# Two attention layers with memory and two gated FFNs on one core: one p-times-v run per unit, weights by columns, eight pooled PSUM banks, and a new order

## The chip, the core and the metric

The kernel runs on one core of one Trainium2 chip. A core has five engines with a queue each: TensorE (PE, its weight loader shown as PEld), VectorE (DVE), ScalarE (ACT), GpSimd (POOL) and SyncE (SP, which issues most DMAs). An engine takes its instructions in the order of its queue; semaphores hold an instruction back until what it needs is there. The metric is device time in microseconds (us), the median of several runs.

## The reference

The input is one sequence of S = 2048 rows of D = 512 numbers. Two layers follow each other, each an attention block A and a feed-forward block B with residuals; both layers use the same weights.

```
x = x + A(layernorm(x));  x = x + B(layernorm(x))      # twice

A: q, k, v = x@wq, x@wk, x@wv        # 32 heads of 16, 4 segments of 512 rows
   per segment s and head:
     p     = softmax(q k^T * scale + causal mask)      # inside the segment
     a_dot = p @ v
     a_mem = (phi(q) @ M) / (phi(q) @ z + 1e-6)        # M, z: of the segments before
     o     = g * a_mem + (1 - g) * a_dot
     M, z  = M + phi(k)^T v, z + sum(phi(k))           # phi(t) = t+1 if t > 0 else exp(t)
   return o @ wo
B: return (silu(x@w_gate) * (x@w_up)) @ w_down         # 512 -> 1792 -> 512
```

## The kernel before, in words

**Precision.** A product of two matrices is made of three matmuls of a faster 32-bit kind: each operand is split in a high and a low part (ACT copies the high part, DVE or POOL subtracts), and high x high, high x low and low x high are added in PSUM (`mm3`, matmuls at line 282). p times v and the memory update run in full 32 bits (four passes).

**Attention.** A layer has 4 segments x 4 groups of 8 heads x 2 halves = 32 units of four heads, `u = 0..31`. Per group, `qk_proj` projects q and k (line 282), ACT copies them to `raw` (468), POOL splits them into the tile `nat` (469, 471), and SP writes `nat` to DRAM (483, 484), from where `load3` brings it back per unit with heads side by side (`cq`, `ck`, lines 508, 513). Per unit there are then:

- `mx_units`: scores for the row maxima. For each of four heads, three fills of a PSUM bank `pmx` (line 531; key widths 256 and 256 in one bank, then 384, then 512), each followed by a masked maximum on DVE (538). `fin` transposes the 16 columns of maxima (547), and ACT sends them by DMA into a row of `cq` (549).
- `at_units`: ten transposed score blocks of 128 keys x 128 queries for four heads (`lt`, line 575, bank `plt`); ACT takes the exponential into tiles `p0`, `p1`, `pc` (581), POOL zeroes the upper triangle of the four diagonal blocks (585); then p times v.
- `pv`, lines 590 to 609: the array is used as four groups of 32 columns (mode "cols"), one head each. `pv(0)` does the first row of key blocks, 512 columns; `pv(1)` the remaining 384 + 128 + 256. Between the two stand three more score blocks. DVE transposes and scales the result (616 to 620).

Besides these, per group: `mem_read` (653), `mem_update` (transposes 669, then 16 small matmuls in mode "cols", 681; DVE and POOL add to M, 685 and 689); per segment: layernorm (`ln_pre`, `ln_fin`, transposes at 373), `v_proj` and `wo_proj` (282).

**FFN.** The first and last parts of the hidden dimension are done plainly (`up`, 975, `down`, 1049); the others by a scheme that needs seven instead of eight block products (`strassen`, 1005), with combinations of weights made on POOL (858, 872) and of inputs on DVE (`make_t`, 919). `down` adds to the residual on DVE (1054).

**Order.** Nothing runs in the order of the code. Each operation is recorded with an engine, a cost and a priority (`at(...)` sets it; the tables `OFF`, `PRE`, `EP`, `PAIR`, `STEP` shift kinds of work against each other, in units of 15 to 17 us), and `Program.issue` (148) then plays all engines: at each step it issues the operation with the lowest priority number among those that its model holds ready, where `LAT` gives the assumed delay from one engine to another and `DRAIN` the assumed cost of a change of mode on PE. What comes out is the order of each queue. No priority is looked at on the chip.

**PSUM.** Eight banks. Before, each had an owner: three `plt` in turn, two `pmx` in turn, one `ppv`, and two `pj` for all else, of which the planner gives the one that is free first. FFN products use the same names.

**Weights at the start.** `load_w4` (415) loads each of wq, wk, wv, wo in four DMAs of 128 rows x 512 columns and splits each piece. A projection of one group of heads needs 128 columns of all four pieces.

Of the kernel before, what the change touches and what calls it, by code (L numbers as in the profile page):

```python
# [12 lines left out]
OP = mybir.AluOpType  # L13
# [11 lines left out]
NB = 3  # L25
LPW = 3
WOT = ("pmx_0", "pmx_1", "pj", "pj")
EARLY_AT = (23, 25, 26)
PAIR, STEP, WAT, TAT = 13.0, 1.83, -2.5, (-1.0, -0.5)
T3E = "dve"  # L30
FIN = 1.9
WQ1 = -6.0
TA, TF = 15.0, 16.7
OFF = {'qe': (0.481, 1.468), 'at': (0.3, 1.1), 'mx': (-0.666, 0.16), 'lf': (-0.709, -0.318), 'mr': (0.865, 0.781), 'mu': (0.556, 0.139), 'wo': (0.263, 1.746), 'qk': (-0.342, 0.41), 'v': (-0.3, 0.518), 'lp': (0.034, 1.108)}
PRE = {'c': -1.851, 'mb': 0.212, 'lv': -1.7, 'lo': -0.87, 'gate': -1.0, 'v': -1.534, 'dv': 0.12, 'qk1': -1.2, 'mx': -1.0}
EP = {'w': -1.935, 'wn': 0.178, 'ln': -3.0, 'dn': -0.06, 'up': -2.73}
POOL_W = ""
TABLE = 1.28
DRAIN = {("full", "cols"): 0.195, ("cols", "full"): 0.095}
# [3 lines left out]
    pe=dict(pe=0.01, act=0.2, dve=0.2, sp=0.19),  # L43
    act=dict(act=0.22, dve=0.13, pe=0.27, pool=0.2, sp=0.15),
    dve=dict(dve=0.13, act=0.13, pe=0.25, pool=0.16, sp=0.12),
    pool=dict(pool=0.1, dve=0.06, pe=0.13, act=0.1, sp=0.05),
# [4 lines left out]
class Buf:  # L51
    def __init__(self, prog, pool, tag, shape, dtype):
# [4 lines left out]
        self.slot = None  # L57
        self.prev = None
# [9 lines left out]
class Op:  # L68
    __slots__ = ("table", "mode", "post", "eng", "cost", "lat", "fn", "prio", "bufs", "succ", "deps", "ready", "need", "wait", "index")

    def __init__(self, eng, cost, lat, fn, prio, bufs):
        self.eng, self.cost, self.lat, self.fn, self.prio, self.bufs = eng, cost, lat, fn, prio, bufs
        self.mode, self.table, self.post = None, None, 0.0
        self.succ, self.deps, self.ready, self.need, self.wait = [], set(), 0.0, None, 0


class Program:
# [19 lines left out]
    def op(self, eng, cost, fn, reads=(), writes=(), lat=0.0):  # L97
# [38 lines left out]
        for b in touch:  # L136
# [3 lines left out]
            if b.tag in self.shared:  # L140
                o.need = b
# [6 lines left out]
    def issue(self):  # L148
        for b in {id(b): b for o in self.ops for b in o.bufs if b.tag in self.shared}.values():
# [15 lines left out]
        held = {tag: [] for tag in self.shared}  # L165
        for o in self.ops:
            if o.wait == 0:
                heapq.heappush(fut[o.eng], (o.ready, o.index, o))
        done, bus, table, mode = 0, 0.0, "exp", "full"
        while done < len(self.ops):  # L170
            best = None
            for e in engs:
                f, n = fut[e], now[e]
                while True:
# [3 lines left out]
                    if n:  # L178
                        o = n[0][2]
                        b = o.need  # L180
                        if b is not None and b.slot is None:
                            if not free[b.tag]:
                                heapq.heappop(n)
                                held[b.tag].append(o)
                                continue
                            fr = min(free[b.tag])
                            if fr[0] > t[e] + 1e-9:
                                heapq.heappop(n)
                                o.ready = fr[0]
# [18 lines left out]
            b = o.need  # L208
            if b is not None and b.slot is None:
# [36 lines left out]
def infini_swiglu(ctx: ExitStack, tc: tile.TileContext, x, wq, wk, wv, wo, beta, wg, wu, wd, out,  # L246
# [149 lines left out]
    def attention(lay, x_in, x_out, slots, T, hook):  # L396
# [7 lines left out]
        def at(v):  # L404
            P.prio = base + v * T
# [800 lines left out]
```

## Time and profile before

| | us |
|---|---|
| median of 3 runs | 1937.13 (1933.95 to 1937.19) |
| span of the profiled execution | 1931.2 |
| PE busy | 1870.8 |
| DVE busy | 1406.9 |
| POOL busy | 905.9 |
| ACT busy | 873.0 |

The profiled execution is known by its span, from its first instruction to its last; the 5.9 us between it and the median of the runs are what lies around the span and what runs differ by. In a group's row stand: the line, the engine, the operation, what it writes and reads, the shapes, the count, then busy time and the mean of one in ns, then the idle time of the engine just ahead of it and what ended that. The first layer's attention fills about 0 to 530 us, its FFN to about 970, then the same again.

### The profile page before, as it was taken

What the parts mean: (1) busy time and instruction counts of PE and PEld (TensorE: products, weight loads), DVE (VectorE), ACT (ScalarE), POOL (GpSimd) and SP (SyncE); (2) the same over time, 40 slices, a digit from 0 to 9 for tenths busy, and PEclk for the clock granted to TensorE, in tenths of its full rate; (3) what the DMA queues carried; (4) which work ended last, traced back from release to release, by engine and by line L of the source; (5) the groups of instructions that cost most, each with busy time, mean ns of one, the idle gap of its engine ahead of it and who ended that gap; (6) DMA issues with size and microseconds to landing.
All of it is one profiled execution on the core that took longest, in us unless ns stands there. A gap on an engine that the chain in (4) does not pass through costs nothing.

```text
span 1931.2 us, 32319 instructions
## 1 busy us (share of the span) xinstructions
PE 1870.8 (97%) x11104; PEld 1437.2 (74%) x11104; DVE 1406.9 (73%) x3834; ACT 873.0 (45%) x1634; POOL 905.9 (47%) x1185
## 2 busy tenths in 40 slices
PE   7999999999989999999999999999999999999999
PEld 5677677776668887788867777777766788878887
DVE  5877867778777668766777678777797756686656
ACT  4555454555624343334326555555455334333332
POOL 5333443444546553655534334444355365455461
PEclk9999999999999999999999999999999999999999
DMA  7433434456131122221364344344561321221121
GB/s 235 135 111 124 132 116 146 129 151 195 45 136 50 55 72 82 71 61 44 95 215 121 102 133 132 116 149 132 152 188 39 131 66 44 87 77 51 44 60 44
DMA packets 120819, 206.09 MB, mean 107 GB/s; under 512 B 14160, under 2 KB 43856, under 8 KB 120656
## 3 DMA queue, kind: packets, MB, share of 16 engines
q1 hardware_dynamic: 118608, 203.49, 34.8%
q8 instruction: 89, 1.46, 0.3%
q10 hardware_dynamic: 2048, 0.53, 0.1%
q14 instruction: 74, 0.61, 0.1%
HBM read 136.34 MB, written 67.11 MB: 105 GB/s over the span
## 4 chain that ended last, share of the span: by engine, by line
PE 78%; DVE 8%; issue 4%; DMA 4%; POOL 3%; ACT 2%; SPq 0%; ACTq 0%; DVEq 0%; POOLq 0%
PE pj L282 16%; PE pj L1049 14%; PE plt L1005 11%; PE pmx L531 8%; PE pmx L1005 8%; PE ppv L603 7%; PE plt L575 6%; PE ppv L1005 3%; DVE junk L538 2%; DMA ck<-scrk 1%; PE pj L975 1%; PE pj L373 1%; PE pj L653 1%; DMA s<-nm 1%; POOL mem L858 1%
## 5 line engine op out<-in xcount | busy, mean ns | idle before, releaser
L538 DVE CUSTOM_DVE_ANT_0 junk<-pmx,amask 128x128 bf16<-128x128 f32 (+3 forms) x1024 | 458.7, 484 | 116.9 <-PE pmx L531 112.0
L282 PE MATMUL pj<-s,s 128*128 128x512 f32 x1416 | 488.2, 410 | 4.9 <-DVE s L1054 4.5
L1049 PE MATMUL pj<-s,vt 128*128 128x512 f32 x1296 | 414.4, 398 | 7.1 <-DVE s L1054 4.5
L581 ACT ACTIVATE s<-plt 128x512 f32<-128x512 f32 x512 | 284.2, 601 | 141.3 <-PE plt L575 133.3
L282 PEld LDWEIGHTS pj<-s,s 128*128 128x128 f32 x1416 | 263.9, 190 | 71.4 <-issue 24.9
L531 PE MATMUL pmx<-ck,s 127*128 127x256 f32 (+2 forms) x1024 | 299.1, 347 | 16.9 <-DVE mx L538 9.5
L1005 PE MATMUL plt<-s,s 128*128 128x512 f32 x1008 | 296.2, 396 | 3.4 <-ACT tt L1020 2.3
L1049 PEld LDWEIGHTS pj<-s,vt 128*128 128x128 f32 x1296 | 243.5, 189 | 68.9 <-DVE s L1054 8.0
L1054 DVE TENSOR_TENSOR s<-s,pj 128x512 f32<-128x512 f32 x224 | 152.9, 684 | 137.9 <-PE pj L1049 137.7
L575 PE MATMUL plt<-s,ck 128*128 128x256 f32 x1280 | 241.6, 288 | 4.2 <-DMA s<-nm 2.1
L531 PEld LDWEIGHTS pmx<-ck,s 127*128 127x128 f32 x1024 | 178.7, 190 | 88.8 <-DVE mx L538 27.0
L1005 PE MATMUL pmx<-s,s 128*128 128x512 f32 x720 | 239.2, 396 | 3.6 <-ACT s L871 2.4
L575 PEld LDWEIGHTS plt<-s,ck 128*128 128x128 f32 x1280 | 211.2, 189 | 32.7 <-ACT s L581 8.5
L1005 PEld LDWEIGHTS plt<-s,s 128*128 128x128 f32 x1008 | 189.6, 189 | 50.4 <-ACT tt L1020 2.7
L585 POOL TENSOR_SCALAR_AFFINE_SELECT s<-s 128x512 f32<-128x512 f32 x192 | 126.9, 664 | 186.5 <-ACT s L581 180.1
L1005 PEld LDWEIGHTS pmx<-s,s 128*128 128x128 f32 x720 | 135.5, 189 | 36.4 <-ACT s L871 3.2
L603 PE MATMUL ppv<-s,vt 128*32 128x512 f32 (+2 forms) x1536 | 136.8, 458 | 0.0
L872 POOL TENSOR_TENSOR s<-mem,s 128x512 fp32r<-128x512 f32 x96 | 126.4, 1318 | 0.0
L469 POOL TENSOR_SCALAR s<-raw 128x512 fp32r<-128x512 f32 x64 | 39.9, 624 | 181.0 <-ACT raw L468 180.6
L1005 PE MATMUL ppv<-s,s 128*128 128x512 f32 x288 | 112.8, 394 | 0.0
L879 POOL COPY turn<-vt 128x1 f32<-128x1 f32 x20 | 3.7, 184 | 230.0 <-DVE vt L962 230.0
L581 ACT ACTIVATE pc<-plt 128x512 f32<-128x512 f32 x128 | 76.8, 600 | 63.8 <-PE plt L575 62.5
(197 smaller groups left out, 2872.5 us busy)
## 6 DMA issues: line engine op xcount, KB each, us to landing
s<-scrq SPq DMA_DIRECT2D x128, 192.0 KB, 3.5
ck<-scrk SPq DMA_DIRECT2D x128, 192.0 KB, 4.5
scrq<-s SPq DMA_DIRECT2D x32, 512.0 KB, 3.0
scrk<-s SPq DMA_DIRECT2D x32, 512.0 KB, 3.1
scrq<-s SPq DMA_DIRECT2D x32, 256.0 KB, 2.0
scrk<-s SPq DMA_DIRECT2D x32, 256.0 KB, 2.0
xin<-xmid SPq DMA_DIRECT2D x32, 256.0 KB, 2.7
s<-xmid SPq DMA_DIRECT2D x32, 256.0 KB, 5.4
```

The lines of the kernel that those rows point to most:

```text
L282: pe(n, passes, lambda: nc.tensor.matmul(view(ps.ap), lhsT=av(a.ap), rhs=bv(b.ap), start=start, stop=stop), [(a, rk[0]), (b, rk[1])], [ps])
L469: gp(0.59, lambda: nc.gpsimd.tensor_scalar(out=nat.ap[:, a, 0, :], in0=raw.ap, scalar1=1.0, scalar2=0.0, op0=OP.mult, op1=OP.add), [raw], ...
L531: nc.tensor.matmul(ps.ap[:, a * 256:a * 256 + nk], lhsT=cq.ap[0:127, 2 * j + p, qt * 128:(qt + 1) * 128], rhs=ck.ap[0:127, p, 0:nk], start ...
L538: dve(w, lambda a=a, qt=qt, w=w, ps=ps, junk=junk: nc.vector.tensor_tensor_reduce(out=junk.ap[:, :w], in0=ps.ap[:, a * 256:a * 256 + w], i ...
L575: nc.tensor.matmul(ps.ap[:, 256 * p:256 * p + 256], lhsT=ck.ap[:, p, kt * 128:kt * 128 + 128], rhs=cq.ap.rearrange("r (j p) c -> r p j c", ...
L581: act(512, lambda: nc.scalar.activation(Pb.ap[:, x].rearrange("p i c -> p (i c)"), ps.ap, AF.Exp, scale=SCALE), [ps], [(Pb, x)], table="exp")
L585: gp(0.593, lambda: nc.gpsimd.affine_select(out=Pb.ap[:, x], in_=Pb.ap[:, x], pattern=[[0, 4], [1, 128]], compare_op=OP.is_ge, fill=0.0, b ...
L603: nc.tensor.matmul(ps.ap[32 * i:32 * i + 32, q0:q0 + w], lhsT=vt.ap[:, kt, VW * hd:VW * hd + 32], rhs=f_[sl].ap[:, b0:b0 + w // 128, idx], ...
L872: gp(n / 400, lambda hi=hi, lo=lo, src=src: nc.gpsimd.tensor_sub(lo(), src(), hi().bitcast(F32)), [read, (wt, (o0, 0))], [(wt, (o0, 1))])
L1005: pe(512, 1, lambda i=i, kc=kc, x=x, buf=buf, view=view: nc.tensor.matmul(ps.ap, lhsT=w.ap[:, o, i, kc], rhs=view(buf.ap, kc), start=(x == 0),
L1049: pe(512, 1, lambda i=i, j=j, fi=fi, x=x, ps=ps, wt=wt, cs=cs: nc.tensor.matmul(ps.ap, lhsT=ht.ap[:, 0:2048].rearrange("p (f a c) -> p f a ...
L1054: dve(512, lambda ps=ps, t=t: nc.vector.tensor_add(xb.ap[:, t, :], xb.ap[:, t, :], ps.ap), [ps, (xb, t)], [(xb, t)])
```

## The change

**p times v.** One operation per unit. It issues after all ten score blocks and does the first row of blocks and the rest in one run. To let two units overlap, even units keep the first row in `p0`; odd units put it in two other places: blocks 0 and 1 in the second slot of `nat`, blocks 2 and 3 in a new tile `pb`, so that the first row's 512 columns become two matmuls of 256 in odd units. `nat` is then one tile per layer whose first slot serves q and k in turn (k of the first two groups excepted). The 16 matmuls of a memory update are no longer an operation of their own: `mem_update` leaves them in the list `MU`, and the next `pv` takes them along.

```diff
-                pe(sum(e[2] for e in parts), 4, go, ..., [ps], mode="cols")
+                runs = (((0, 0, 2), (0, 2, 2)) if u % 2 else ((0, 0, 4),)) + ((1, 1, 3), (3, 3, 1), (2, 2, 2))
...
+                    for f, _, _ in MU_:
+                        f()
...
+                pe(1280 + 100 * len(MU_), 4, go, [(vt, c) for c in range(8)] + reads + [e[1] for e in MU_],
+                   [ps] + [e[2] for e in MU_], mode="cols")
...
-            units = [lt(0, q) for q in range(4)] + [lt(1, q) for q in (1, 2, 3)] + [pv(0)]
-            units += [lt(2, 2), lt(3, 3), lt(2, 3), pv(1)]
+            units = [lt(0, q) for q in range(4)] + [lt(1, q) for q in (1, 2, 3)]
+            units += [lt(2, 2), lt(3, 3), lt(2, 3), pv]
```

On PE, in the first layer, the run of an odd unit. Before (`ppv` is the bank of p times v, `pmx` of maxima, `plt` of score blocks, `pj` of the rest), first half, then, 22 rows on, second half:

```order
L531 MATMUL pmx_3376<-ck_99,s_67 128x384
L282 MATMUL pj_3311<-s_2911,s_218 128x512
L603 MATMUL ppv<-s_3270,vt_88 32x512 x4
L282 MATMUL pj_3311<-s_2911,s_218 128x512
L531 MATMUL pmx_3389<-ck_99,s_67 128x512
```

```order
L575 MATMUL plt_3467<-s_238,ck_256 128x256 x2
L282 MATMUL pj_3471<-s_2898,s_191 128x512
L603 MATMUL ppv<-s_3340,vt_88 32x384 x4
L603 MATMUL ppv<-s_3340,vt_88 32x128 x4
L603 MATMUL ppv<-pc,vt_88 32x256 x4
L282 MATMUL pj_3471<-s_2898,s_191 128x512
```

And of the change (lines 295, 558, 609, 636 and 718 are the former 282, 531, 575, 603 and 681; every bank is now called `ps`):

```order
L558 MATMUL ps_3191<-ck_100,s_67 128x512
L295 MATMUL ps_3182<-s_285,s_2732 128x512
L609 MATMUL ps_3199<-s_241,ck_266 128x256 x2
L295 MATMUL ps_3182<-s_285,s_2732 128x512
L636 MATMUL ps_3209<-s_271,vt_88 32x256 x4
L636 MATMUL ps_3209<-pb,vt_88 32x256 x4
L636 MATMUL ps_3209<-s_3103,vt_88 32x384 x4
L636 MATMUL ps_3209<-s_3103,vt_88 32x128 x4
L636 MATMUL ps_3209<-pc,vt_88 32x256 x4
L718 MATMUL ps_3210<-vt_88,of 32x34 x16
L573 MATMUL ps_3252<-ident,mx_3123 16x128
```

The two halves and the memory update, which stood apart, are one run. Over the whole program, runs of this kind of matmul fall from 150 to 64.

**PSUM.** All eight banks are one pool; an operation that opens a bank takes any free one, as long as its class holds fewer than its cap.

```diff
+CAP = {'pj': 3, 'plt': 3, 'pmx': 3, 'ppv': 3, 'ff': 6, 'st': 6}
...
-    P = Program({"pj": 2})
+    P = Program({"ps": 8})
```

`st` is the start of the first layer, `ff` the FFN's products. On PE, a stretch of scores for maxima, with bank numbers, before (`pmx_0`, `pmx_1`; the last number is that of the buffer):

```order
L531 MATMUL pmx_1_3781<-ck2_256,s16_238 128x256 x2
L531 MATMUL pmx_0_3786<-ck2_256,s16_238 128x384
L575 MATMUL plt_2_3791<-s14_67,ck0_99 128x256 x2
L282 MATMUL pj_1_3801<-s4_2898,s0_191 128x512
L575 MATMUL plt_0_3803<-s14_67,ck0_99 128x256 x2
L603 MATMUL ppv_3809<-s12_3693,vt1_88 32x512 x4
L531 MATMUL pmx_1_3817<-ck2_256,s16_238 128x512
L531 MATMUL pmx_0_3819<-ck2_256,s16_238 128x256 x2
```

and of the change:

```order
L558 MATMUL ps_2_3494<-ck2_266,s16_241 128x512
L295 MATMUL ps_4_3458<-s4_2732,s3_118 128x512
L609 MATMUL ps_5_3501<-s14_67,ck0_100 128x256 x2
L295 MATMUL ps_4_3458<-s4_2732,s3_118 128x512
L558 MATMUL ps_1_3506<-ck2_266,s16_241 128x256 x2
L295 MATMUL ps_4_3458<-s4_2732,s3_118 128x512
L558 MATMUL ps_6_3513<-ck2_266,s16_241 128x384
L295 MATMUL ps_4_3458<-s5_2791,s2_115 128x512
L609 MATMUL ps_3_3518<-s14_67,ck0_100 128x256 x2
L295 MATMUL ps_4_3458<-s5_2791,s2_115 128x512
L558 MATMUL ps_7_3524<-ck2_266,s16_241 128x512
```

Before, scores came in pairs that alternate between two banks; now single fills stand between projection matmuls, in banks 2, 1, 6 and 7.

**Weights by columns.** `load_w` and `load_w4` load wq and wk in pieces of 128 columns of all 512 rows, one per group of heads, with priorities of their own (`w1` to `w3`); wv and wo stay by rows. A projection of group n waits for piece n alone.

```diff
+        def wcols(nm, w, n):
+            if nm in "qk":
+                return w[:, n * 128:(n + 1) * 128].rearrange("(k p) c -> p k c", p=128)
+            return w[n * 128:(n + 1) * 128, :].rearrange("(k p) c -> p k c", p=128)
```

SP's queue at the start, before:

```order
L348 DMA tt_69<-in_A_x_dram 128x512
L348 DMA tt_75<-in_A_x_dram 128x512
L348 DMA phiq_80<-in_A_x_dram 128x512
L348 DMA phiq_91<-in_A_x_dram 128x512
L420 DMA s_95<-in_A_wq_dram 128x512 x4
L420 DMA s_107<-in_A_wk_dram 128x512 x4
L420 DMA s_129<-in_A_wv_dram 128x512 x4
```

and of the change:

```order
L450 DMA s_69<-in_A_wq_dram 128x4x128
L450 DMA s_75<-in_A_wk_dram 128x4x128
L362 DMA tt_80<-in_A_x_dram 128x512
L362 DMA tt_91<-in_A_x_dram 128x512
L362 DMA phiq_95<-in_A_x_dram 128x512
L362 DMA phiq_97<-in_A_x_dram 128x512
L450 DMA s_69<-in_A_wq_dram 128x4x128
L450 DMA s_75<-in_A_wk_dram 128x4x128
```

The first column pieces of wq and wk now go ahead of x, the others behind it.

**The order set anew.** All numbers of the planner are new: the shifts (`OFF`, now one table per layer, `PRE`, `EP`, `PAIR`, `STEP`, `FIN` and others), the costs of a mode change, and the assumed delays between engines, all 1.45 times the former ones but those of SP.

```diff
-    pe=dict(pe=0.01, act=0.2, dve=0.2, sp=0.19),
+    pe=dict(pe=0.01, act=0.29, dve=0.29, sp=0.27),
```

Since the shifts move nearly every row of every queue, the excerpts above stand for them. Also new: one `junk` tile for the outputs of the maxima that nobody reads, instead of two; and one of the four first layernorms ends on POOL instead of ACT.

254 lines of the change are left out of this document (141 added, 113 removed).

## The prediction

> **What bounds the kernel now.** The page of the profile first: its first line, and the busy time of the engines.
>
> ```profile
> span 1931.2 us, 32319 instructions
> PE 1870.8 (97%) x11104; PEld 1437.2 (74%) x11104; DVE 1406.9 (73%) x3834; ACT 873.0 (45%) x1634; POOL 905.9 (47%) x1185
> ```
>
> TensorE (PE) is busy for 97% of the span; nothing else is near. So the time is the work of PE plus what PE loses, and a busy share alone hides part of the loss: a matmul that starts late because its weights were loaded late still counts as busy. I therefore work out PE's own work from counts and steps, and call the rest lost. The table by stretches gives the step of a 128x512 matmul where nothing disturbs it (the first row), and the stages behind it.
>
> ```profile
> 600.00:700.00 100.00, 100.00 (x434) 80.98 (x433) 62.61 (x96) 35.63 (x63) 58.45 (x64) 1.00 0.20 58
> 0.00:75.00 75.00, 60.69 (x313) 44.81 (x314) 50.43 (x169) 35.60 (x67) 36.21 (x65) 0.95 0.63 198
> 75.00:525.00 450.00, 439.00 (x3353) 325.20 (x3352) 343.90 (x1279) 242.91 (x473) 195.14 (x296) 1.00 0.44 130
> 1000.00:1440.00 440.00, 433.08 (x3291) 323.00 (x3289) 334.88 (x1259) 232.92 (x459) 181.97 (x273) 1.00 0.46 137
> ```
>
> 434 matmuls in 100.00 us are 0.2304 us each. The columns are length, then busy time and count of PE, PEld, DVE, ACT, POOL, then the granted clock. In the attention of the two layers (the third and fourth rows) DVE is busy 76% and PE 98%. The groups give the counts of the other forms, and the order of time their steps.
>
> ```profile
> L531 PE MATMUL pmx<-ck,s 127*128 127x256 f32 (+2 forms) x1024 | 299.1, 347 | 16.9 <-DVE mx L538 9.5 <-DMA ck<-scrk 5.0 <-DVE of L635 0.5
> L575 PE MATMUL plt<-s,ck 128*128 128x256 f32 x1280 | 241.6, 288 | 4.2 <-DMA s<-nm 2.1 <-ACT s L581 1.5
> L603 PE MATMUL ppv<-s,vt 128*32 128x512 f32 (+2 forms) x1536 | 136.8, 458 | 0.0
> L603 PE MATMUL ppv<-pc,vt 128*32 128x256 f32 x512 | 39.4, 379 | 0.0
> L373 PE MATMUL pj<-ident,xn 128*128 128x128 f32 x240 | 40.3, 275 | 2.4 <-POOL xn L365 2.4
> L653 PE MATMUL pj<-mb,phiq 128*128 128x136 f32 x160 | 29.8, 286 | 1.1 <-DVE s L378 0.6 <-ACT nm L549 0.5
> L669 PE MATMUL pj<-ident,phik 128*128 128x128 f32 x96 | 23.1, 271 | 0.0
> L630 PE MATMUL pj<-ident,mem 128*128 128x128 f32 x96 | 20.4, 273 | 0.0
> L547 PE MATMUL pj<-ident,mx 128*16 128x128 f32 x64 | 17.4, 273 | 1.2 <-DVE of L635 1.0
> L681 PE MATMUL pj<-vt,of 128*32 128x34 f32 x768 | 11.2, 198 | 0.0
> ```
>
> ```profile
> 252.61 0.40 PE L531 MATMUL pmx<-ck,s 127*128 127x256 f32 x2
> 252.85 0.67 PE L653 MATMUL pj<-mb,phiq 128*128 128x136 f32 x4
> 253.26 0.42 PE L531 MATMUL pmx<-ck,s 127*128 127x384 f32 x1
> ...
> 255.90 0.42 PE L282 MATMUL pj<-s,s 128*128 128x512 f32 x1
> 256.25 1.07 PE L603 MATMUL ppv<-s,vt 128*32 128x384 f32 x16
> 257.13 0.61 PE L603 MATMUL ppv<-pc,vt 128*32 128x256 f32 x8
> 257.68 3.72 PE L282 MATMUL pj<-s,s 128*128 128x512 f32 x15
> ...
> 280.51 1.07 PE L603 MATMUL ppv<-s,vt 128*32 128x512 f32 x8
> 281.51 0.73 PE L531 MATMUL pmx<-ck,s 127*128 127x512 f32 x3
> ```
>
> Reading starts against starts: a 256-column matmul steps 0.12 us (two in 0.24), a 136-column one 0.10. The second half of p times v runs from 256.25 to 257.68, 1.43 us, the first half from 280.51 to 281.51, 1.00 us, and the L282 matmul ahead of a run takes 0.35 us instead of about 0.24: entering the column mode costs **0.11 us**. Leaving it is inside the 1.43 us: the last eight matmuls take 0.55 us, where 256 columns by four passes at 0.2304/512 us per column would be 0.46, so **0.09 us**. An enter and a leave together are 0.20 us.
>
> The sum of PE's work: 1280 of L575 at 0.12 are 153.6 us. The 1024 of L531 are 256 heads of 256, 256, 384 and 512 columns, 0.24 + 0.173 + 0.2304 = 0.643 each, 164.7. The 2048 of L603 are 64 units (32 records each) at 2.43, 155.5; entering happens 128 times for them and 24 times for the memory updates (768 records of L681, 32 each), 152 x 0.11 = 16.7, and their own 11.2. The five groups of transposes and memory reads above hold 656, and 48 more lie in three small groups: 704 at about 0.11, 77.4. What is left of 11104 is 5280 matmuls of 512 columns at 0.2304, 1216.5. Together **1795.6 us; lost are 135.6 us** of the span.
>
> Where they are lost, from further stretches and from the waits:
>
> ```profile
> 36.00:49.30 13.30, 9.64 (x62) 7.18 (x61) 6.00 (x26) 2.38 (x4) 5.90 (x12) 0.75 0.99 268
> 536.00:547.70 11.70, 7.66 (x26) 5.57 (x25) 11.00 (x16) 2.38 (x4) 3.42 (x3) 0.85 0.24 90
> 778.00:786.60 8.60, 6.03 (x18) 3.94 (x18) 7.05 (x10) 4.00 (x7) 8.60 (x9) 0.80 0.41 123
> 972.00:984.60 12.60, 8.47 (x23) 5.93 (x24) 8.65 (x15) 4.45 (x7) 4.38 (x5) 0.73 0.82 243
> 1728.00:1735.50 7.50, 4.93 (x13) 3.17 (x14) 5.71 (x7) 2.88 (x6) 7.50 (x8) 0.78 0.35 105
> ```
>
> ```profile
> PEld pmx L531 <- DVE mx L538: 27.0, 53, 1.3
> PEld plt L575 <- ACT s L581: 8.5, 24, 0.8
> ```
>
> (a) The start, 0 to 75: 14.3 us idle, and slow matmuls at 36 to 49 (clock 0.75) and while weights trickle in, some 20 us. (b) Four holes at the borders of attention and FFN: 26 matmuls are 6.0 us of 11.7, and likewise 4.5 of 8.6 lost, 7.3 of 12.6, 4.5 of 7.5, together 22 us; a hole is paid twice, since the granted clock falls after it. (c) The end, some 4. (d) The rest, **90 us**, is short waits. Those for a bank of scores stand out: 9.5 us of idle PE (row L531 above) and 27.0 us of weight loads held back, 53 times, mean 0.51.
>
> **The change part by part.** *One run of p times v, the memory update inside it.* Before, PE enters the column mode for 64 x 2 halves and 24 updates, two of which adjoin a half: 150 runs. In the new order 64 are left (the 53 lone transposes of maxima, with 16 columns, stand alone in both). 86 x 0.20 = **17 us off**, all on PE's path. Its ends: 86 x 0.11 = 9 if only entering counts, and 86 x 0.5 = 43 if the whole idle time of the weight loader around a run did. I take 17, read from starts. Each odd unit splits 512 columns in two of 256, 4 more matmuls; same columns, and at most 32 x 0.11 = 3.5 us; I take none.
>
> By the Trainium skill, "TensorEngine Tiling (Array Packing)", Key Properties, a change of the tiling mode drains the array, and "TensorE: Matmul & The Clock Gate", Single matmul latency, puts a drain at about 175 ns; two drains on each of 86 runs would be an estimate of 30 us, and the time 13 us below mine. The starts above show 0.20 for both together, so the measurement decides.
>
> *Eight banks with caps.* Scores may hold three banks instead of two. The reduce that frees one is
>
> ```profile
> L538 DVE CUSTOM_DVE_ANT_0 junk<-pmx,amask 128x128 bf16<-128x128 f32 (+3 forms) x1024 | 458.7, 484 | 116.9 <-PE pmx L531 112.0
> ```
>
> 0.48 us, about the mean of the 53 waits, so one bank more outlasts most of them; DVE has the room (76% busy). Banks of projections go from two to three as well, but all caps draw on the same eight.
>
> *The order.* The planner now assumes handovers 1.45 times as long (PE to ACT 0.29 for 0.2), so it puts a consumer further behind its producer. In the second excerpt four score fills in a row go to four banks, where before every second fill came back to the same bank. What the old small margins cost is (d); its bounds are 0 and 90 us kept. I take **26 kept**, under a third: the named bank waits (36.5) mostly go, and the rest thins out by the wider margins. Nearest to the kept part are the stretches that already run so: 600 to 700 loses nothing.
>
> *The start.* 512 columns of weights by rows are replaced by 128-column groups, so the first projection of q no longer waits for four pieces of wq:
>
> ```profile
> 13.31 7.10 PE L282 MATMUL pmx<-s,s 128*128 128x512 f32 x19 [0.68 <-ACT s L377]
> ```
>
> 19 matmuls take 7.1 us there, 2.7 too long. But two weight DMAs now go ahead of x on SP, which delays PE's first matmul by about their issues (0.9 us), and k's bank now waits until POOL has split q. I take (a) from 20 to 17, ends 13 and 25. Holes (b): the DVE work at the borders is the same, 11.00 of 11.7 us busy; better placed, half stays, 11, ends 4 and 22. The end stays 4.
>
> *One slot of `nat` for q and k.* POOL's split must wait until the DMA has read the former one, and POOL's masks of the diagonal stand behind it in the queue. Projections come once per unit, some 14 us apart (the 450 us of the third row above for some 32 units), and the copy is short:
>
> ```profile
> scrq<-s SPq DMA_DIRECT2D x32, 512.0 KB, 3.0
> ```
>
> So it costs nothing, or 3 us at each of the few places where two projections adjoin.
>
> **Sum.** 1795.6 - 17 = 1778.6 of work, plus 17 + 11 + 4 + 26 = 58 lost: span 1836.6. The profiled execution's span lies 5.9 us below the median of the runs (1937.13 against 1931.2), so the time is **1842 us**.
>
> **The rivals.** *Only the switches come*: the new order loses as much as the old at other places, since DVE, with the same 344 us in a shorter attention, is at 83% and in bursts full. For it speaks the hole at 536, where DVE is busy 11.00 of 11.70 us; against it, that the waits are short and many elsewhere. Time 1937 - 17 = 1920. Chance 0.12.
>
> *Nearly all stalls go*: (a) 14, (b) 6, (c) 4, (d) 8: 1778.6 + 32 + 5.9 = 1816, and with the dearer switch down to 1800. For it, the undisturbed FFN stretch. Chance 0.14.
>
> *Slower: PE waits at the single run.* It now needs all ten exponentials and the four masks of its unit before its first column, while the first half before needed only the upper row of blocks. The masks and what POOL may be doing ahead of them are
>
> ```profile
> L585 POOL TENSOR_SCALAR_AFFINE_SELECT s<-s 128x512 f32<-128x512 f32 x192 | 126.9, 664 | 186.5 <-ACT s L581 180.1 <-DMA ck<-scrk 4.5 <-PE pj L373 0.3
> L471 POOL TENSOR_TENSOR s<-raw,s 128x512 fp32r<-128x512 f32 x64 | 84.3, 1317 | 3.8
> ```
>
> An exponential (0.6), a mask (0.66) and a split ahead (1.32) make 2.6 us; at all 64 runs that is 166 us, 2008 in all. It turns slower from about 1.5 us per run (95 us over 64). Against it: the last score blocks are issued rows ahead of the run, with projection matmuls between. Chance 0.07.
>
> *More holes with the low clock.* A wait that grows past some 4 us costs a second time. The stretch right after the hole at 536 shows it:
>
> ```profile
> 544.00:547.70 3.70, 3.70 (x11) 2.88 (x10) 3.04 (x6) 1.14 (x2) 0.00 (x0) 0.54 0.40 143
> ```
>
> 11 matmuls take 3.7 us instead of 2.5. Ten new holes of 4 us with 1.2 us behind each would give 1842 + 52 = 1894. Chance 0.07. The Trainium skill, "TensorE: Matmul & The Clock Gate", What's actually happening, halves the clock after an idle window of about 3.4 us; by that rule, the trace agrees (0.54).
>
> **How the numbers follow.** Forecast 0.60, nearly all 0.14, only switches 0.12, more holes 0.07, slower 0.07. The range 1808 to 1892 takes in the ends of (a), (b) and the switch, and (d) from 8 to 66; it leaves out the rival of 1920, the slower one and the lowest part of the better one. A measurement of this kernel tells about 0.2% from no change; faster by more than that has 0.91, the same 0.02, slower 0.07.
>
> **What would show it.** In the new profile: idle PE well under half of 60 us; the waits of L531's successor (line 558) for DVE under 10 us in PE and PEld together; about 64 idle gaps "issue" at the weight loader before line 636 instead of 166; PE's work by the same sum near 1779; clock below 0.9 in fewer stretches. I am wrong if PE waits for POOL at line 636, if DVE is full for long stretches, or if the holes at the FFN's borders grow.

## The result and the profile after

The changed kernel takes 1985.09 us (median of 4 runs, 1982.16 to 1988.93) where the kernel before, on the same chip, takes 1937.16: a ratio of 1.0257, 95% interval 1.0241 to 1.0273. (The ratios here are formed from the single runs and differ by up to 0.1% from the quotient of two medians.) It is slower by 48 us; the forecast was 1842, faster by 95. What follows finds the miss in one tile that the prediction gave no price, the single `junk`.

The first lines of the page of the changed kernel:

```profile
span 1983.4 us, 33072 instructions
PE 1867.4 (94%) x11360; PEld 1458.7 (74%) x11360; DVE 1461.1 (74%) x3834; ACT 880.6 (44%) x1629; POOL 907.3 (46%) x1186
```

PE's idle time, span less busy, went from 60.4 to 116.0 us. DVE's count is the same, 3834, but it is busy 54 us longer. The waits of the changed kernel (engine, what it works on, what it waited for, us in total, times, longest) name the place:

```profile
PEld ps L636 <- issue: 51.1, 212, 0.7
PEld ps L573 <- DVE mx L564: 33.5, 29, 2.7
PE ps L573 <- DVE mx L564: 32.0, 35, 2.4
PEld ps L558 <- DVE mx L564: 23.5, 65, 1.2
PEld ps L609 <- DVE mx L564: 14.7, 35, 1.6
PE ps L558 <- DVE mx L564: 14.2, 38, 1.0
...
PEld ps L636 <- POOL s L619: 2.6, 8, 0.7
```

Three kinds of PE work now wait for the maxima of line 564 (538 before): their transposes (573), the fills of scores (558), and the score blocks (609). Before, the fills were the only ones of them with more than 3 us of such waits, 9.5 on PE and 27.0 on the loader. The last row is the rival in which PE waits for POOL's masks at the single run: 2.6 us in all.

Why are the maxima late? The group's row of the reduces in the changed kernel (busy, mean ns, idle time of DVE just ahead and what ended it):

```profile
L564 DVE CUSTOM_DVE_ANT_0 junk<-ps,amask 128x128 bf16<-128x128 f32 (+3 forms) x1024 | 499.8, 488 | 136.5 <-PE ps L558 43.1 <-PE ps L609 0.5 <-PE ps L295 0.5
```

The mean of one is what it was, 488 ns for 484. Two other numbers moved: busy rose by 41 us, and of 136.5 us of idle time ahead of the reduces only 44 have a releaser. Before, 112.0 of 116.9 had one. Some 92 us of waiting are thus put down to nobody. The order of time on DVE shows what they are (start, duration):

```profile
249.84 0.29 DVE L564 CUSTOM_DVE_ANT_0 junk<-ps,amask 128x128 bf16<-128x128 f32 x1
250.06 0.08 DVE L564 DVE_READ_ACCUMULATOR2_ANT mx<- 128x1 f32 x1
250.18 0.42 DVE L564 CUSTOM_DVE_ANT_0 junk<-ps,amask 128x256 bf16<-128x256 f32 x1
250.53 0.08 DVE L564 DVE_READ_ACCUMULATOR2_ANT mx<- 128x1 f32 x1
250.75 0.56 DVE L564 CUSTOM_DVE_ANT_0 junk<-ps,amask 128x384 bf16<-128x384 f32 x1
251.24 0.08 DVE L564 DVE_READ_ACCUMULATOR2_ANT mx<- 128x1 f32 x1
251.46 0.69 DVE L564 CUSTOM_DVE_ANT_0 junk<-ps,amask 128x512 bf16<-128x512 f32 x1
252.08 0.08 DVE L564 DVE_READ_ACCUMULATOR2_ANT mx<- 128x1 f32 x1
252.31 0.29 DVE L564 CUSTOM_DVE_ANT_0 junk<-ps,amask 128x128 bf16<-128x128 f32 x1
```

From one reduce to the next, the starts are 0.34, 0.57, 0.71 and 0.85 us apart; the four of one head take 2.47 us. Each begins only after the one ahead of it has ended (250.18 after 249.84 + 0.29, and so on).

### The profile page after: what moved, and what is told of

The parts are those of the page before. It is cut to its first block, busy times and chain, and to the rows that moved or that the text cites. A ratio compares the mean times of both kernels' runs of the same rounds, so it can differ in the third digit from the quotient of the medians.

```text
span 1983.4 us, 33072 instructions
## 1 busy us (share of the span) xinstructions
PE 1867.4 (94%) x11360; PEld 1458.7 (74%) x11360; DVE 1461.1 (74%) x3834; ACT 880.6 (44%) x1629; POOL 907.3 (46%) x1186
## 4 chain that ended last, share of the span: by engine, by line
PE 42%; DVE 11%; issue 3%; DMA 2%; POOL 2%; ACT 1%; SPq 0%; DVEq 0%; ACTq 0%; POOLq 0%
PE ps L1047 16%; PE ps L1091 10%; PE ps L295 6%; DVE junk L564 5%; PE ps L558 3%; PE ps L609 3%; PE ps L636 2%; DMA s<-nm 1%; PE ps L1017 1%; DVE tt L961 1%; PE ps L387 0%; DVE s L983 0%; DMA ck<-scrk 0%; DVE bst L367 0%; DVE vt L1004 0%
## 5 line engine op out<-in xcount | busy, mean ns | idle before, releaser
L564 DVE CUSTOM_DVE_ANT_0 junk<-ps,amask 128x128 bf16<-128x128 f32 (+3 forms) x1024 | 499.8, 488 | 136.5 <-PE ps L558 43.1
L1047 PE MATMUL ps<-s,s 128*128 128x512 f32 x2016 | 551.7, 397 | 11.4 <-ACT s L982 6.2
L295 PE MATMUL ps<-s,s 128*128 128x512 f32 x1536 | 530.5, 410 | 7.8 <-ACT s L451 3.9
L1047 PEld LDWEIGHTS ps<-s,s 128*128 128x128 f32 x2016 | 379.1, 189 | 104.5 <-ACT s L982 8.8
L1091 PE MATMUL ps<-s,vt 128*128 128x512 f32 x1296 | 377.2, 396 | 0.8 <-ACT vt L1003 0.8
L615 ACT ACTIVATE s<-ps 128x512 f32<-128x512 f32 x448 | 252.6, 603 | 192.3 <-PE ps L609 136.9
L295 PEld LDWEIGHTS ps<-s,s 128*128 128x128 f32 x1536 | 289.9, 192 | 53.5 <-ACT s L451 4.3
L558 PE MATMUL ps<-ck,s 127*128 127x256 f32 (+2 forms) x1024 | 292.2, 343 | 20.5 <-DVE mx L564 14.2
L1091 PEld LDWEIGHTS ps<-s,vt 128*128 128x128 f32 x1296 | 243.6, 188 | 58.6 <-ACT vt L1003 1.4
L609 PE MATMUL ps<-s,ck 128*128 128x256 f32 x1280 | 252.8, 291 | 12.9 <-DMA s<-nm 6.2
L609 PEld LDWEIGHTS ps<-s,ck 128*128 128x128 f32 x1280 | 219.0, 190 | 50.4 <-DVE mx L564 14.7
L558 PEld LDWEIGHTS ps<-ck,s 127*128 127x128 f32 x1024 | 181.7, 191 | 69.1 <-DVE mx L564 23.5
L1017 PE MATMUL ps<-s,s 128*128 128x512 f32 x384 | 127.6, 406 | 0.0
L1017 PEld LDWEIGHTS ps<-s,s 128*128 128x128 f32 x384 | 73.1, 191 | 17.8 <-issue 1.2
```

Source lines behind the costliest of these rows:

```text
L295: pe(n, passes, lambda: nc.tensor.matmul(view(ps.ap), lhsT=av(a.ap), rhs=bv(b.ap), start=start, stop=stop), [(a, rk[0]), (b, rk[1])], [ps])
L558: nc.tensor.matmul(ps.ap[:, a * 256:a * 256 + nk], lhsT=cq.ap[0:127, 2 * j + p, qt * 128:(qt + 1) * 128], rhs=ck.ap[0:127, p, 0:nk], start ...
L564: dve(w, lambda a=a, qt=qt, w=w, ps=ps: nc.vector.tensor_tensor_reduce(out=junk.ap[:, :w], in0=ps.ap[:, a * 256:a * 256 + w], in1=amask.ap ...
L609: nc.tensor.matmul(ps.ap[:, 256 * p:256 * p + 256], lhsT=ck.ap[:, p, kt * 128:kt * 128 + 128], rhs=cq.ap.rearrange("r (j p) c -> r p j c", ...
L615: act(512, lambda: nc.scalar.activation(view().rearrange("p x i c -> p (x i c)"), ps.ap, AF.Exp, scale=SCALE), [ps], [(Pb, key)], table="exp")
L1017: pe(512, 1, lambda i=i, j=j, kc=kc, x=x, ps=ps, wt=wt: nc.tensor.matmul(ps.ap, lhsT=wt.ap[:, i, kc, cs], rhs=XT[b][j].ap[:, :, kc], start ...
```

## The experiments

**Theory A: the single `junk`.** With two tiles in turn, a reduce may start while the one ahead of it still writes. With one, it must wait for that write: in the trace 937 of the 1024 reduces of the changed kernel wait for a semaphore of DVE itself, which in a burst is raised by the read of the accumulator of the reduce ahead; with two tiles 253 do. **Rival B:** the waits come from the new order, banks and runs, whatever the reduces write.

*Two tiles in the changed kernel.* To make room, two small buffers (`nm`, `r`) become single ones; every queue has the order of the changed kernel, row for row.

```diff
-    junk = sb("junk", [128, 512], BF16)
+    junks = [sb(f"junk{i}", [128, 512], BF16) for i in range(2)]
...
+                            junk = junks[njunk[0] % 2]
+                            njunk[0] += 1
```

> The changed kernel with two tiles in turn for the outputs of the row-maximum reduces that nobody reads (junk), where it has one; to make room, two tiny double buffers (nm, r) become single. The order of every queue is that of the changed kernel, row for row. Theory A (one junk tile makes each reduce wait until the one ahead of it has written, 0.12 to 0.23 us longer from start to start; DVE falls behind, and the transposes of the maxima on PE wait for it): the reduces step 0.21, 0.34, 0.48, 0.62 us again, the waits of line 573's successor for DVE fall from 32 us to under 8, and the time from 1985 to 1850 to 1900 us. Theory B (the single run of p times v, the pooled banks and the new order cost the time, and DVE's longer steps are only waits for PE): within 10 us of 1985. Theory C (both): 1900 to 1960.

Measured: 1875.34 us (1873.37 to 1877.59), ratio to the kernel before 0.9681, interval 0.9664 to 0.9697. The one tile cost the changed kernel 110 us. The same place in the order of time, with two tiles:

```profile
250.06 0.29 DVE L568 CUSTOM_DVE_ANT_0 junk<-ps,amask 128x128 bf16<-128x128 f32 x1 [3.71 <-PE ps L560]
250.27 0.08 DVE L568 DVE_READ_ACCUMULATOR2_ANT mx<- 128x1 f32 x1
250.27 0.42 DVE L568 CUSTOM_DVE_ANT_0 junk<-ps,amask 128x256 bf16<-128x256 f32 x1
250.62 0.08 DVE L568 DVE_READ_ACCUMULATOR2_ANT mx<- 128x1 f32 x1
250.62 0.55 DVE L568 CUSTOM_DVE_ANT_0 junk<-ps,amask 128x384 bf16<-128x384 f32 x1
251.10 0.08 DVE L568 DVE_READ_ACCUMULATOR2_ANT mx<- 128x1 f32 x1
251.10 0.69 DVE L568 CUSTOM_DVE_ANT_0 junk<-ps,amask 128x512 bf16<-128x512 f32 x1
251.71 0.08 DVE L568 DVE_READ_ACCUMULATOR2_ANT mx<- 128x1 f32 x1
251.71 0.29 DVE L568 CUSTOM_DVE_ANT_0 junk<-ps,amask 128x128 bf16<-128x128 f32 x1
```

Now a reduce starts 0.07 to 0.08 us before the one ahead has ended, and the head takes 1.65 us for 2.47. Page, group and waits of this kernel:

```profile
span 1875.9 us, 33042 instructions
PE 1824.0 (97%) x11360; PEld 1457.0 (78%) x11360; DVE 1402.2 (75%) x3834; ACT 874.2 (47%) x1629; POOL 911.7 (49%) x1186
```

```profile
L568 DVE CUSTOM_DVE_ANT_0 junk<-ps,amask 128x128 bf16<-128x128 f32 (+3 forms) x1024 | 436.9, 482 | 57.8 <-PE ps L560 56.2
```

```profile
PEld ps L577 <- DVE mx L568: 2.5, 6, 0.8
PEld ps L560 <- DVE mx L568: 2.2, 5, 1.2
PE ps L577 <- DVE mx L568: 0.8, 3, 0.4
PE ps L560 <- DVE mx L568: 0.8, 4, 0.3
```

Nearly all idle time ahead of the reduces has a releaser again (56.2 of 57.8). The reduces occupy DVE 63 us less by busy time and 91 us less by idle time without a releaser, 154 us in all. The waits at lines 558 and 573 (here 560 and 577) fall from 103 to 6 us.

*One tile in the kernel before*, the order of its queues unchanged, all outputs nobody reads in one tile:

```diff
+    J = sb("jone", [128, 512], BF16)
...
-                                out=junk.ap[:, :w], in0=ps.ap[:, a * 256:a * 256 + w], in1=amask.ap[:, 512 - w:],
+                                out=J.ap[:, :w], in0=ps.ap[:, a * 256:a * 256 + w], in1=amask.ap[:, 512 - w:],
```

> The kernel before with all junk outputs of the reduces put into one tile; its queues keep their order row for row. Theory A: slower, 1937 to 1980 or more, the steps of reduces that follow a reduce longer by 0.12 to 0.23 us. Theory B: within 8 us of 1937.

Measured: 1985.0 us (1984.05 to 1986.21), ratio 1.0251, interval 1.0236 to 1.0266. One tile alone costs the kernel before 49 us. Its group's row:

```profile
L539 DVE CUSTOM_DVE_ANT_0 jone<-pmx,amask 128x128 bf16<-128x128 f32 (+3 forms) x1024 | 499.5, 488 | 141.4 <-PE pmx L532 73.0 <-PE plt L576 0.5 <-DVE mx L539 0.2
```

The same signature: busy up by 41, and 68 us of idle time without a releaser. So A holds from both sides, and B falls. In this order 680 of 1024 reduces follow a reduce directly, against 828 in the new one; by busy time and idle time without a releaser the tile costs DVE 104 us here and 154 there.

*One tile, but an order that knows the price.* Could the planner have hidden it?

```diff
-        op("dve", n / 960 / fast + 0.0687, fn, reads, writes)
+        op("dve", n / 960 / fast + 0.0687 + more, fn, reads, writes)
...
-                                [(ps, a), amask], [(junk, (lay, u, p, j, qt)), (mx, (qt, p, j))])
+                                [(ps, a), amask], [(junk, (lay, u, p, j, qt)), (mx, (qt, p, j))], more=0.12 if w == 128 else 0.23)
```

> The changed kernel with its one junk tile; only the planner's price of a reduce is raised by what a write wait adds (0.12 us at 128 columns, 0.23 above), so that the order is set with it. 811 reduces still follow a reduce directly, for 828. Theory A (the wait is a loss of VectorE's capacity, and in attention VectorE is then full, so no order recovers it): within 25 us of 1985, 1960 to 1990. Rival (the loss is that of an order that does not know of the wait): more than half of the 110 us comes back, below 1930.

Measured: 1976.53 us, ratio 1.0219 (1.0195 to 1.0243), against 1.0257 (1.0241 to 1.0273). It recovers about 9 of the 110 us, and the two intervals touch. So the rival falls for this planner; that no order could do it is not shown. The new order also loses more to the clock: the mean granted clock is 0.985 for 0.990, by an estimate from these and the spans some 30 us for 20. That DVE is full, as theory A put it, is not shown by this: in the changed kernel its windows over attention have

```profile
75.00:525.00 450.00, 418.92 (x3362) 320.83 (x3362) 348.67 (x1248) 234.11 (x453) 176.25 (x272) 0.99 0.44 128
1000.00:1440.00 440.00, 407.40 (x3137) 309.96 (x3136) 326.37 (x1154) 216.19 (x418) 163.43 (x250) 0.99 0.45 129
```

and 675 us busy with the 92 unaccounted make at most 86% of 890. It is the burst of reduces that takes half as long again, and PE's fills and transposes stand behind it.

**The switches.** Is a leave-and-enter pair of the column mode worth 0.20 us? The kernel with two tiles, with one matmul of zeros more per run: in its middle, where it forces a switch, or at its end, where one comes anyway.

```diff
+                        if kt == 3:
+                            nc.tensor.matmul(ps.ap[:, 0:128], lhsT=amask.ap[:, 0:128], rhs=amask.ap[:, 0:128], start=False, stop=False)
```

> The kernel of e1_two_junk with one 128-column matmul more in the middle of each of the 64 runs of p times v: it multiplies zeros into the run's bank and uses all rows of the array, so that TensorE leaves the column mode and enters it again once per unit. The output is the reference's. Theory A (a leave-and-enter pair costs about 0.20 us, as the trace of before has it, and the extra matmul about 0.06): 64 x 0.26 = 17 us more than e1_two_junk's 1875, so 1888 to 1895. Rival (the switch is hidden beside the weight loads and only the matmul's own columns count): 2 to 5 us more, below 1881. e4_switch_end tells what the extra matmul costs without the switch.

```diff
-                                             start=(x == 0), stop=(x == len(parts) - 1))
+                                             start=(x == 0), stop=False)
...
+                    nc.tensor.matmul(ps.ap[:, 0:128], lhsT=amask.ap[:, 0:128], rhs=amask.ap[:, 0:128], start=False, stop=True)
```

> The kernel of e1_two_junk with the same extra matmul of zeros at the end of each run of p times v, where TensorE leaves the column mode anyway (10 pairs of switches are added, where the next run followed at once). The output is the reference's. Both theories: 64 x 0.06 and 10 x 0.20 = 4 to 6 us more than e1_two_junk, 1879 to 1881. The difference of e3_switch_mid to this run is 54 pairs of switches: 11 us by 0.20 each, nothing by the rival.

Measured: middle 1885.11 us, ratio 0.9746 (0.9731 to 0.9761); end 1872.74, ratio 0.9685 (0.9667 to 0.9703). The middle lies between the two theories, 10 us above the kernel with two tiles where A had 13 to 20. The end lies below the 1879 to 1881 of both; by the ratios it is 0.8 us above the kernel with two tiles, and the two intervals are too wide to exclude 4 us. The difference of the two is 12.4 us; by the two intervals together, 7 to 16 us. The traces show the price directly. One run with the matmul in its middle:

```profile
231.59 1.71 PE L642 MATMUL ps<-s,vt 128*32 128x512 f32 x16
233.23 0.23 PE L637 MATMUL ps<-amask 128*128 128x128 bf16 x1
233.39 0.43 PE L642 MATMUL ps<-s,vt 128*32 128x128 f32 x8
233.64 0.62 PE L642 MATMUL ps<-pc,vt 128*32 128x256 f32 x8
234.18 0.50 PE L296 MATMUL ps<-s,s 128*128 128x512 f32 x1
```

From its first matmul to the next of another kind it takes 2.59 us. With two tiles alone the same run takes 2.29 us, with the matmul at its end 2.33. Over the 64 runs the median is 0.30 us more in the middle, 19 us in all, and 0.04 at the end (0.04 to 0.07, by what follows), some 4 us in all. The ten runs that are followed at once by a transpose of maxima with 16 columns pay 0.07 at the end and not the price of a pair. So no pair is added there, and the difference is that of 64 pairs and not of the 54 that were expected. A pair then costs 0.23 to 0.26 us by the traces, and 0.19 by the times (0.11 to 0.25). PE's busy time, from the first lines of the two pages, middle and then end, where the kernel with two tiles has 1824.0:

```profile
PE 1839.4 (97%) x11424; PEld 1455.4 (77%) x11424; DVE 1403.4 (74%) x3834; ACT 872.8 (46%) x1629; POOL 909.4 (48%) x1186
```

```profile
PE 1820.2 (97%) x11424; PEld 1454.4 (78%) x11424; DVE 1401.3 (75%) x3834; ACT 873.4 (47%) x1629; POOL 910.6 (49%) x1186
```

So the weight loads do not hide the switch, and the rival falls. Of the 19 us that the runs grew in the middle the time shows 10 by the medians and 13 by the ratios; what takes up the rest is not explained here.

**Banks, delays, the single run.** All on the kernel with two tiles, with the order set anew by the planner; differences are to its 1875.34 us (the kernel before, run beside each, took 1934.99 to 1936.34).

Two banks for scores in place of three (`'pmx': 3` to `'pmx': 2` in `CAP`):

> The kernel of e1_two_junk with a cap of two PSUM banks for the scores whose maxima are taken, in place of three; the planner sets the order anew. Theory A (the third bank is what lets TensorE go on past a late maximum): the short waits come back by a good part of the 40 us that e1_two_junk lost less than the kernel before: 10 to 30 us more than 1875, so 1885 to 1905. Rival (the delays in the planner's table alone do it, the third bank is hardly needed): within 5 us of 1875.

Measured: 1902.58 us, 0.9834 (0.9820 to 0.9849), 27 us more. The time is that of theory A, but its mechanism does not show: the fills of scores (560) wait 5.0 us for the maxima, PE and loader together, where with three banks they wait 3.0. Four banks (`'pmx': 4`):

> The kernel of e1_two_junk with a cap of four banks for the scores whose maxima are taken, the order set anew. Theory A (the third bank already outlasts the reduces): within 8 us of 1875. Rival (the waits that are left would go with a bank more, as they did from two to three): 8 to 20 us less, 1855 to 1867.

Measured: 1897.21 us, 0.9804 (0.9781 to 0.9828), 22 us more: neither theory. The former delays (all `LAT` but SP's back to `0.2` for `0.29`, and so on):

> The kernel of e1_two_junk with the planner's delays between engines as they stood before (about two thirds of the new); the order is set anew with them. Theory A (the longer delays keep a distance between VectorE's reduces and the matmuls that need their banks): 10 to 25 us more than 1875, 1885 to 1900, as more short waits at the scores' banks. Rival (the banks do it and the delays are only a way of counting): within 5 us of 1875.

Measured: 1915.31 us, 0.9904 (0.9882 to 0.9925), 40 us more, beyond theory A; the same waits are 9.9 us. Delays 1.3 times as long again:

> The kernel of e1_two_junk with the planner's delays 1.3 times as long again. Theory A (the delays only buy distance, and the waits of VectorE's banks are gone from e1_two_junk already, 0.8 us each): within 8 us of 1875. Rival (the 60 us of short losses that are left are still margins that are too small): 8 to 25 us less, 1850 to 1867.

Measured: 1889.57 us, 0.9763 (0.9739 to 0.9788), 14 us more: neither theory. The expected direction came out for the first of each pair, but the opposite step costs 14 to 22 us as well. So these four do not price a bank or a delay. The likely reason, which no run separates, is that any other value upsets an order whose shifts fit this one. What can be said is the sum, with caps like the former owners and the former delays together:

```diff
-CAP = {'pj': 3, 'plt': 3, 'pmx': 3, 'ppv': 3, 'ff': 6, 'st': 6}
+CAP = {'pj': 2, 'plt': 3, 'pmx': 2, 'ppv': 1, 'ff': 6, 'st': 6}
...
-    pe=dict(pe=0.01, act=0.29, dve=0.29, sp=0.27),
+    pe=dict(pe=0.01, act=0.2, dve=0.2, sp=0.19),
...
```

> The kernel of e1_two_junk with the old delays and with caps that repeat the former owners (projections 2, transposes and score blocks 3, scores for maxima 2, p times v 1), the order set anew: what stays of the change is the single run of p times v with its memory updates, the weights by columns and the one pool. Theory A (the runs are worth about 17 us, banks and delays the rest, and they overlap): 1936 less 17, so 1912 to 1928, the time of the rival in which only the switches come. Rival (the banks and delays already gave all that e5_cap_two and e6_old_delays lost, 28 and 40 us, one upon the other): 1875 and 68, 1940 to 1950.

Measured: 1928.41 us, 0.9957 (0.9942 to 0.9971): 7 us below the kernel before, at the edge of theory A, and the rival falls. From there to 1875 are 53 us, but the shifts are still the new ones, so this run too has an upset order: its mean granted clock is 0.985 for 0.992, by an estimate from these and the spans some 14 us more lost to the clock, and its score blocks (613) wait 17.1 us on PE for the DMA of the maxima, for 5.7. So 53 us are caps and delays and what the order loses without them; how it divides stays open, and the run gives no price for the single run of p times v either.

**The start.** The first pieces of wq and wk behind x:

```diff
-PRE = {'w1': -6.063, ...
+PRE = {'w1': -1.99, ...
```

> The kernel of e1_two_junk with the first weight pieces of wq and wk queued behind the four loads of x on SP, and not ahead of them; else the order near the start is set anew by that. Theory A (the first transpose of TensorE waits for the x that stands behind two weight loads; 9.6 us against 6.65 in the kernel before): the first matmul comes 2.5 to 3 us earlier and the time is 2 to 4 us less than e1_two_junk. Rival (the first projection then waits for its weights, and the gain is given back): within 1 us of e1_two_junk.

Measured: 1875.91 us, 0.9686 (0.9670 to 0.9702): the rival. PE's first rows with x first, and then with the weights first:

```profile
6.65 1.11 PE L389 MATMUL ps<-ident,xn 128*128 128x128 f32 x4 [6.65 <-ACT xn L378]
8.17 3.12 PE L389 MATMUL ps<-ident,xn 128*128 128x128 f32 x12 [0.40 <-ACT xn L378]
11.97 2.50 PE L296 MATMUL ps<-s,s 128*128 128x512 f32 x5 [0.68 <-ACT s L393]
```

```profile
9.60 3.67 PE L389 MATMUL ps<-ident,xn 128*128 128x128 f32 x16 [9.60 <-ACT xn L378]
13.95 0.79 PE L296 MATMUL ps<-s,s 128*128 128x512 f32 x1 [0.68 <-ACT s L393]
```

The first transposes come 3 us earlier and the first projection 2, and nothing of it is left at the end.

**What is left of the miss.** With two tiles the kernel still stands 33 us above the forecast. Is that DVE?

```diff
-                                out=junk.ap[:, :w], in0=ps.ap[:, a * 256:a * 256 + w], in1=amask.ap[:, 512 - w:],
+                                out=junk.ap[:, :128], in0=ps.ap[:, a * 256:a * 256 + 128], in1=amask.ap[:, 384:],
```

> The kernel of e1_two_junk in which each of the 1024 reduces reads 128 columns only, so that the maxima of 768 of them are taken over a part of their scores; the order of every queue stays. VectorE has some 200 us less to do in attention (256 x (0.13 + 0.26 + 0.39)). Theory A (the 33 us by which e1_two_junk stands above the forecast are matmuls that start late behind a VectorE that is busy 79% in attention): 15 to 35 us less than 1875, 1840 to 1860. Rival (what is left is lost at places where VectorE is not late: the start, transfers, ScalarE, the borders): less than 8 us below, 1867 to 1877.

Measured: 1865.86 us, 0.9643 (0.9626 to 0.9659), 9.5 us less, between the two (by the two ratios 7 us, within the rival). The busy times of its page:

```profile
PE 1812.8 (97%) x11360; PEld 1452.9 (78%) x11360; DVE 1238.1 (66%) x3834; ACT 871.9 (47%) x1629; POOL 912.8 (49%) x1186
```

164 us of DVE work went and about a quarter of the 33 us with it. Once the reduces overlap, DVE is no longer what holds most of it. The fastest kernel that computes all of the reference is the one with two tiles, and those that differ from it by the matmul of zeros at the end of a run or by the start, which can't be told from it.

## Why the prediction was wrong, point by point

**The step that failed: the reduces' cost, "DVE has the room (76% busy)".** The prediction took 0.48 us for a reduce, from the mean of its row, and let a third bank outlast it. What counts in a burst is the distance from start to start, and the single `junk` moved it. By all starts of the two traces, a reduce followed directly by a reduce steps as follows (median of before, then after):

| columns | before, us | after, us | such pairs after |
|---|---|---|---|
| 128 | 0.212 | 0.334 | 237 |
| 256 | 0.345 | 0.576 | 223 |
| 384 | 0.477 (lower quartile) | 0.710 | 210 |
| 512 | 0.617 | 0.843 | 158 |

The pairs times the lengthening are 29 + 52 + 49 + 36 = 165 us more of DVE's time, close to the 154 that the group's rows gave. The tile stood in the list of what is new; it got neither a price nor a rival. The term that was missing is 110 us, and it alone turns the sign. The other half of the step, that a third bank is what outlasts the waits, is not shown either: with two tiles the fills of scores wait 3.0 us for DVE, with a cap of two banks 5.0, and with the former caps and delays together 4.3, where the kernel before had 36.5. What took these waits away lies in the rest of the new order.

**The work of PE, 17 us less: right, but its level too high.** By starts against starts over all matmuls, with the lower quartile of each form (and of the form that follows) as its undisturbed step, PE's work falls by about 20 us from before to the kernel with two tiles, and what PE loses between its first and last matmul goes from about 160 to 122 us; the first matmul comes 3 us later. These sum to the 55 us between the two spans. In the changed kernel, by the same steps, some 230 us are lost. The work of the kernel before is some 1760 us by this count, where the prediction's sum has 1795.6; the largest part of the difference are the 704 short matmuls, put at 77.4 us, which take 65.5 from start to start with all their late ones. So its "lost" terms are too small by that much as a whole, and only their changes can be compared. The split of 512 columns in two of 256 cost nothing, as taken: odd runs take 2.30 us, even ones 2.29. The price of a switch pair is 0.23 to 0.26 by the traces of the added matmuls, where 0.20 was read from starts. By the Trainium skill, "TensorE: Matmul & The Clock Gate", Single matmul latency, two drains would be an estimate of 0.35; the runs give less.

**(d), 26 us kept: right in kind for the named waits, too low in size.** With two tiles, the scores' waits that the prediction named, 36.5 us, are 3. But the span of 1875.9 stands 39 us above the forecast's 1836.6 (the profiled execution is one of the longer ones; the median of the runs stands 33 us above). By starts, (d) fell from some 117 to 84 us, by 33 where the forecast took off 64; this is 31 of the 39. The holes, next point, are 12; the start fell by 2 for 3, the end stayed at 4, and the work fell by a few us more than forecast. Some 515 matmuls come 0.06 to 0.2 us late, 52 us together, where in the kernel before some 700 did, 70 us: this kind thinned out by a quarter only. With less work for the reduces it is still 47 us. Its cause stays open.

**(b), holes, 11 us kept: wrong.** Places where the clock falls, in windows of the kernel with two tiles (last columns: granted clock, DMA share, GB/s):

```profile
751.00:763.00 12.00, 9.45 (x35) 7.20 (x34) 9.24 (x16) 2.94 (x5) 8.91 (x13) 0.86 0.44 123
939.00:951.00 12.00, 10.00 (x40) 7.79 (x40) 6.75 (x20) 3.71 (x6) 5.19 (x8) 0.86 0.74 244
1055.00:1067.00 12.00, 9.81 (x66) 8.29 (x59) 6.70 (x28) 6.82 (x13) 4.36 (x6) 0.86 0.40 108
1382.00:1394.00 12.00, 9.77 (x75) 8.20 (x75) 10.48 (x40) 7.42 (x14) 6.93 (x11) 0.86 0.56 131
1441.00:1455.00 14.00, 10.36 (x35) 7.95 (x34) 10.57 (x18) 4.11 (x8) 0.00 (x0) 0.76 0.23 75
```

There are five, some 23 us by starts, for four with 22 before. The holes at 536 and 1728 went, one came at the start of the second FFN (1441), and two came inside the second attention (1055, 1382). These two are waits of score blocks for the DMA that brings the row of maxima, which the prediction did not name:

```profile
PE ps L613 <- DMA s<-nm: 5.7, 3, 2.2
```

"A wait that grows past some 4 us costs a second time" puts the length too high. In the two traces the longest single idle time of PE in each of the four and the five holes is 1.7 to 4.0 us, and behind each the granted clock falls to 0.5 for 3.4 or 6.8 us; other idle times of 1.8 us have no such fall behind them.

**(a), 20 to 17 us: the change about right, the reason wrong.** By starts the start loses 24 us for 26, of which the later first matmul takes 3 back. The weights ahead of x delay PE's first matmul by 3 us and not by 0.9; the time doesn't depend on it. (The two pieces that go ahead are those of the second group of heads, not of the first, as the planner's priority w1 says.)

**`nat` in one slot at nothing: no run speaks against it.** In the kernel with two tiles POOL waits once for such a read, and PE waits less than before (1.7 us for 5.0) for the scores' transfer:

```profile
POOL s L494 <- DMA scrq<-s: 4.6, 1, 4.6
```

**The signs named.** About 64 gaps "issue" at the weight loader ahead of line 636 were forecast; there are 212, and 208 with two tiles. So those gaps do not count switches: 176 of the 212 lie inside a run. Idle PE was to be well under half of 60 us; with two tiles it is 52. The clock was to be below 0.9 in fewer stretches; apart from the end there were five before, and there are six with two tiles and ten with one. The rivals: the slower one, PE waiting for POOL, did not come (2.6 us). "Only the switches come" named DVE in bursts, which was the right place, but priced it from the trace of two tiles.

## What to carry to other kernels

An output that nobody reads is still a buffer: give it two slots, or count the write wait for every operation that follows its like. Such a wait shows neither in the mean of one nor among the named waits; look at the distance from start to start in a burst, and at idle time ahead of a group that no releaser explains. When a planner's table was fitted to one setting, a change of one number measures the upset order too, so a part's worth can't be read from it alone.

## What was not expected of the hardware

Two reduces on DVE overlap by 0.07 to 0.08 us at their border when they write different tiles; the read of the accumulator (0.08 us) begins together with the next reduce. When they write the same tile, the next starts 0.12 us later after 128 columns and 0.23 us later after 256 to 512. The two sizes come from the number of waits, as the trace shows, and not from the columns as such. The reduce behind one of 128 columns reads the same bank, so it waits for DVE's own semaphore alone and starts 0.04 us after the read of the accumulator has ended (median of 236). The others wait for PE's semaphore as well; the wait for DVE's own then stands ahead of them as an instruction by itself, and they start 0.14 us after the read (median of 589).

The Trainium skill, "VectorE: DVE Perf Modes", The DRAIN you can't avoid, says that the next operation does not start until the pipeline has emptied, though one that is not held starts earlier, and that in eight copies a semaphore after each cost nothing more. The two excerpts in the order of time agree with the exception and differ from the last: without the wait the 256-column reduce starts at 250.27, before the one of 250.06 + 0.29 has ended, and the wait makes four reduces take 2.47 us for 1.65.

Taking 164 us of busy time off DVE moved the time by 9.5 us; 154 us of write waits on the same engine had moved it by 110. What an engine's time is worth is not one price: in the first case the reduces kept up with PE already, in the second they did not.
